# Cosine attention and a two-layer network on one core: the first chunk's second products in pairs of groups, and w_out loaded by whole rows

## The chip, the cores and the metric

The kernel runs on one core of a Trainium2 chip. The metric is the device time of one execution in microseconds (us); a profiled execution also gives a trace, whose span runs from the first to the last instruction. The engines of the core are named as in the profile: PE (matrix products, with PEld for the loading of weights), DVE (vector), ACT (activations), POOL (GpSimd), SP (which here only issues DMAs). Each runs its own instructions in order, and waits on semaphores for the others.

## What is computed

```python
q_n = q / (norm(q) + 1e-6);  k_n = k / (norm(k) + 1e-6)      # (8, 12, 448, 64)
attn = softmax(q_n @ k_n.T / 0.1)
x = (attn @ v).transpose(0, 2, 1, 3).reshape(3584, 768)
h = x @ w_in                                                  # (768, 2048)
out = maximum(0.01 * h, h) @ w_out                            # (2048, 768)
```

All inputs and the output are float32 in memory; the products run in bfloat16.

## The kernel before

**Slots.** Two heads make a slot, so a batch has 6 slots and there are 48 in all. A slot's q and k are loaded by SP (`load_qk`: four DMAs, the last two small; the first six slots by `load_first`), squared on POOL (`squares`, L184), summed on DVE (`sums`, L195), turned into norms on ACT (`roots`, L202 and L203), and scaled on DVE (`normalise`, L222 to L227). Its seven tiles are then transposed, on PE for slots below 10 and by a DMA on SP from slot 10 on (`transposes`, L259). `norm(s)` is roots, normalise, transposes, the load of a later slot, and the squares of slot s+2. `hold(x)` is a tiny copy on POOL that reads x, so what follows on POOL stands behind x.

**Scores and attention.** `key_tiles` makes one score tile (a pair of PSUM banks, L284) for each slot and key tile, and ACT takes its exp out of the banks (L296). `attend` and `attend_two` multiply the exps with v and with ones and scale the result into xT.

**The two layers.** A batch is a chunk of tokens (3 or 4 tiles of 128). `firsts` makes the 16 parts of the hidden layer (L388), each through one bank, with a Prelu on ACT into hT (L395). `visit` makes the second products (`two_groups`, L460): a group is one token tile and one half (384) of the 768 columns. Two groups run together in two banks, one on rows 0 to 63 of the contraction and one on rows 64 to 127; after all 16 m they change rows. A yield after each m (a step) lets `visit` put score tiles of the next batch and norms of later slots between them, at fixed steps (`three`, `four`, `norms`). In the first chunk (b = 0) the pairs are ((0,0),(1,0)), ((2,0),(0,1)), ((1,1),(2,1)), each (token tile, half). The other chunks have pairs ((ts,0),(ts,1)).

**Banks.** PSUM has eight banks. `banks` gives out the single bank or the pair that was used longest ago, apart from those kept for a group or a product.

**Loads.** POOL issues the loads of v, w_in (four) and w_out in the opening (`bulk`); DMAs of one issuing engine share a queue (q0 in the profile is POOL's, q1 is SP's). w_out comes as columns 0 to 383 in two loads of 8 m and then columns 384 to 767 in four loads of 4 m.

**The opening.** Slots 0 to 5 go one by one through squares, sums, roots, normalise, transposes and scores, written out by hand, with filler matmuls (`fill`) between. On POOL the order is: hold for slot 0's q, the first v load, hold for slot 0's remainder, the remainder loads of slots 3 to 5, hold for the scaled slot 0, squares of slot 2. For slots 0 and 1 the 1e-6 is added on ACT by an Identity (L205), for the others on DVE (L222).

The work of PE is one sequence in program order:

```python
attend(NQ - 1, ...); firsts(0, ...)
for b in range(B):
    visit(b, ...)            # second products of b, scores of b + 1
    attend_batch(b + 1)
    firsts(b + 1, 0, ...)
```

Of the kernel before, what the change touches and what calls it, by code (L numbers as in the profile page):

```python
# [8 lines left out]
F32 = mybir.dt.float32  # L9
# [7 lines left out]
def kernel(  # L17
# [10 lines left out]
    nc = tc.nc  # L28
# [47 lines left out]
    def banks(count, keep=None, which=None):  # L76
        lo, hi = (0, 8) if not deals["apart"] else (0, 4) if count == 2 else (4, 8)
        x = which if which is not None else min(
            (i for i in range(lo, hi, count) if not set(range(i, i + count)) & set(sum(kept.values(), []))),
            key=lambda i: max(age[i : i + count]),  # L80
        )
        deals["n"] += 1
        age[x : x + count] = [deals["n"]] * count
        if keep:
            kept[keep] = list(range(x, x + count))
        return ps[:, x] if count == 1 else ps[:, x : x + count]
# [20 lines left out]
            out=w_in_sb[:, e::2, n0 : n0 + D_ff // 2], in_=w_in_r[e, :, :, n0 : n0 + D_ff // 2]  # L107
        )

    def load_w_out(half, parts=1):  # L110
        n0, n = half * HALF, MT // parts
        for m in range(0, MT, n):
            gp.dma_start(
                out=w_out_sb[:, m : m + n, n0 : n0 + HALF],
                in_=w_out_r[:, m : m + n, n0 : n0 + HALF],
            )

    def main(x, b, h0, nh):
        return x[b, h0 : h0 + nh, 0:MAIN].rearrange("h (p t) d -> p h t d", t=3)
# [79 lines left out]
    def roots(s):  # L199
        if s >= NSLOT:  # L200
            return
        nc.scalar.activation(ss[s], ss[s], func=AF.Ln, bias=tiny)  # L202
        nc.scalar.activation(ss[s], ss[s], func=AF.Exp, scale=0.5)  # L203
        if s < 2:
            nc.scalar.activation(ss[s], ss[s], func=AF.Identity, bias=eps)  # L205

    qn, scalings = {}, {}

    def behind(eng, ins, why):

        tc.add_manual_dep(
            eng.nop().ins, ins.ins.name,
            mybir.DependencyInfo(mybir.DependencyClass.Sync, mybir.DependencyReason.DATA),
            reason=why,
        )

    def normalise(s):
        if s >= NSLOT:
            return
        r = smp.tile([128, 14], F32, name="r")  # L220
        if s >= 2:
            nc.vector.tensor_scalar_add(ss[s], ss[s], 1e-6)  # L222
        nc.vector.reciprocal(r, ss[s])  # L223
        qn[s] = qnp.tile([128, 7, 2, D], BF16, name="qn")
        for x, lo, hi, r0 in ((raw[s][0], 0, 4, 0), (raw[s][1], 4, 7, 8)):
            nt = hi - lo
            scalings[s] = nc.vector.tensor_tensor(  # L227
                qn[s][:, lo:hi],
                x.rearrange("p h t d -> p t h d"),
                r[:, r0 : r0 + 2 * nt].rearrange("p (h t) -> p t h", h=2)  # L230
                .unsqueeze(3).to_broadcast([128, nt, 2, D]),
                op=ALU.mult,
            )
# [209 lines left out]

    halves_done = {}

    def two_groups(c, two, last):

        po2 = banks(2, ("rows", c, two))  # L450
        done = {}
        for n in range(2):
            before, done = done, {}
            for m in range(MT):
                for h in range(2):
                    rows, i = slice(64 * h, 64 * h + 64), h ^ n
                    ts, half = two[i]
                    if n == 1 and m == 0:
                        behind(nc.tensor, before[i], "the other rows' products in this bank")
                    done[i] = nc.tensor.matmul(  # L460
                        out=po2[:, i, :HALF],
                        lhsT=hT[c][rows, m, ts * 128 : (ts + 1) * 128],
                        rhs=w_out_sb[rows, m, half * HALF : (half + 1) * HALF],
                        start=(n == 0 and m == 0), stop=(n == 1 and m == MT - 1),
                    )
                yield
        for i, (ts, half) in enumerate(two):
            if (c, ts) not in osb:
                osb[c, ts] = osp.tile([128, D_model], F32, name="osb")
            copy = nc.scalar.copy if last and i == 0 else nc.vector.tensor_copy  # L470
            copy(out=osb[c, ts][:, half * HALF : (half + 1) * HALF], in_=po2[:, i, :HALF])  # L471
            halves_done[c, ts] = halves_done.get((c, ts), 0) + 1
            if halves_done[c, ts] == 2:
                store(osb[c, ts], c, chunk_cols(c)[0] + ts * 128, 0, D_model)
        given_back(("rows", c, two))

    for part in range(2):
        load_first(nc.sync, q, part, 0, 1)
# [5 lines left out]
            load_first(nc.sync, x, part, s, n)  # L484
    tiny = cpool.tile([128, 1], F32, name="tiny")
    nc.vector.memset(tiny, 1e-18)
    eps = cpool.tile([128, 1], F32, name="eps")
    nc.vector.memset(eps, 1e-6)
    warm = cpool.tile([128, 512], BF16, name="warm")
    nc.vector.memset(warm, 1.0)  # L490
    ones = cpool.tile([128, 32], BF16, name="ones")
# [23 lines left out]
        seen = smp.tile([128, 1], F32, name="seen")  # L515
        gp.tensor_copy(out=seen, in_=x)  # L516

    hold(raw0[:, 0, 0, 0, 0:1])
    load_v(0)
    hold(raw0[:, 0, 0, 3, 0:1])  # L520
    for x in (q, k):
        load_first(gp, x, 1, 3, 3)


    (q_h, k_h), (q_h1, k_h1) = raw[0], raw[1]
# [19 lines left out]
    load_v_rem(0, slice(0, 2))  # L545
    dst = qtp.tile([128, 7, 128], BF16, name="qkT")
    qkT[0] = dst.rearrange("p t c -> p (t c)")
    for lo, hi, copy in ((0, 4, nc.scalar.copy), (4, 7, nc.vector.tensor_copy)):
        tp = transposed()
        one(tp, 0, lo, hi)  # L550
        if hi == 7:
            sums(1, (1,))
        copy(out=dst[:, lo:hi], in_=tp[:, lo:hi])
    fill(3)
    sums(1, (0,))
    sums(2, (0,))
    roots(1)
# [2 lines left out]
    def bulk(s):  # L560

        if s == 0:
            load_v(1)
            load_w_in(0)
        elif s == 1:
            load_v_rem(0, slice(2, 4))
            load_w_in(1)
        elif s == 2:
            load_v(2)
            load_w_in(2)  # L570
        elif s == 3:
            load_w_in(3)
            load_w_out(0, 2)
        elif s == 4:
            load_w_out(1, 4)

    def scaled(s):

# [150 lines left out]
    def visit(b, order, norms, between):  # L729


        s0 = (b + 1) * NPAIR
        tiles = [(s0 + p, ki) for p in range(NPAIR) for ki in range(3)]
        key_tiles([(s0 + 1, 3), (s0 + 3, 3)])
        for i, two in enumerate(order):
            after = between[i == len(order) - 1]
            for n, _ in enumerate(two_groups(b, two, i == len(order) - 1), 1):
                for _ in range(after.get(n, 0)):
                    key_tiles([tiles.pop(0)])
                for fn in norms.get((i, n), ()):  # L740
                    fn()
        assert not tiles
        key_tiles([(s0 + 5, 3)])

    three = ({5: 1, 11: 1, 16: 2, 21: 1, 27: 1}, {3: 1, 7: 1, 11: 1, 16: 2, 20: 1})
    four = ({5: 1, 11: 1, 16: 2, 24: 1}, {6: 1, 16: 2})

    deals["apart"] = False
# [16 lines left out]
    for b in range(B):  # L765
        tokens = chunk_cols(b)[1] // 128
        if b == B - 1:
            for ts in range(tokens):
                for half in range(2):
                    second(b, ts, half)  # L770
            break
        order = [((ts, 0), (ts, 1)) for ts in range(tokens)]
        if b == 0:
            order = [((0, 0), (1, 0)), ((2, 0), (0, 1)), ((1, 1), (2, 1))]
        norms = {(0, 16): [lambda: sums(11)], (0, 26): [lambda: norm(11)]}
        if b:
            norms = {}
            for i in range(tokens - 1):
                norms[i, 4] = [lambda s=ready + i: norm(s)]
                norms[i, 20] = [lambda s=ready + i + 1: sums(s)]  # L780
        visit(b, order, norms, three if tokens == 3 else four)
        ready += tokens - 1
        attend_batch(b + 1)
        for j in range((b + 2) * NQ, (b + 3) * NQ):
            load_v(j)
        load_v_rem(b + 2)
        s = ready
        between = {0: [lambda s=s: norm(s)], 1: [lambda s=s: sums(s + 1)]}
        if b == 0:
            between = {  # L790
                0: [lambda: sums(13)], 1: [lambda: norm(13), lambda: sums(14)],
                4: [lambda: norm(14), lambda: sums(15)], 7: [lambda: norm(15)],
                13: [lambda: sums(16)],
            }
            ready += 4
        elif tokens == 3:
            between.update({
                4: [lambda s=s: norm(s + 1), lambda s=s: sums(s + 2)],
                7: [lambda s=s: norm(s + 2), lambda s=s: sums(s + 3)],
                10: [lambda s=s: norm(s + 3)], 13: [lambda s=s: sums(s + 4)],  # L800
            })
            ready += 4
        else:
            between.update({
                4: [lambda s=s: norm(s + 1)], 5: [lambda s=s: sums(s + 2)],
                8: [lambda s=s: norm(s + 2)], 12: [lambda s=s: sums(s + 3)],
            })
            ready += 3
        firsts(b + 1, 0, between)
# [35 lines left out]
```

## Time and profile before

| | us |
|---|---|
| median of 3 runs (lowest, highest) | 409.29 (409.26, 409.75) |
| the profiled execution | 408.97 |
| its span | 407.2 |
| PE busy | 399.3 (98%) |
| ACT busy | 262.6 (64%) |
| DVE busy | 189.8 (47%) |
| POOL busy | 140.7 (35%) |
| second products L460: busy, mean of one | 143.2, 323 ns |
| score exps L296: mean of one | 919 ns |

The durations of the trace come from the one profiled execution; 1.8 us of its time lie outside the span. Where the profile names a wait, the text in square brackets gives the idle time of the engine before an instruction and what ended it. Of two lines of DMA queues, the first number is packets, the second MB written, the third the time that the packets took as a share of 16 DMA engines; several packets can be under way on an engine, so a share can be over 100%.

### The profile page before, as it was taken

How to read it: one execution, taken by the hardware profiler on the slowest of the kernel's cores; microseconds unless marked ns; L12 is line 12 of the kernel's file. 1: busy time of each engine (PE TensorE's matmuls, PEld its weight loads, DVE VectorE, ACT ScalarE, POOL GpSimd, SP SyncE). 2: the span in 40 equal slices, each digit the busy share in tenths (PEclk: the TensorE clock that was granted, in tenths of full speed). 3: DMA queues.
4: the chain of work that ended last, by engine and by line, in shares of the span. 5: the costliest groups of instructions: out<-in, count | busy, mean ns of one | idle time of the engine just before them, and what ended most of it. 6: DMA issues, size and time to landing. Idle time of an engine off the chain costs nothing.

```text
span 407.2 us, 10112 instructions
## 1 busy us (share of the span) xinstructions
PE 399.3 (98%) x4096; PEld 216.3 (53%) x4096; DVE 189.8 (47%) x405; ACT 262.6 (64%) x455; POOL 140.7 (35%) x215
## 2 busy tenths in 40 slices
PE   7899999999999999999999999999999999999996
PEld 2335657544555655544555555544555555554564
DVE  6887951771645624354542635256261645130021
ACT  4996598565865688744876569845876559944300
POOL 4995461471323522343231614055231530000000
PEclk9999999999999999999999999999999999999999
DMA  7999999694595659378385848486476833210033
GB/s 169 263 212 218 222 181 212 194 211 107 134 208 82 142 85 218 65 117 174 78 196 121 131 119 146 130 117 136 93 194 142 111 74 63 63 41 2 0 77 79
DMA packets 104175, 54.21 MB, mean 133 GB/s; under 512 B 70016, under 2 KB 99072, under 8 KB 104128
## 3 DMA queue, kind: packets, MB, share of 16 engines
q1 hardware_dynamic: 78064, 41.04, 43.6%
q0 software_dynamic: 25216, 12.00, 24.0%
q8 instruction: 32, 0.52, 0.6%
q10 hardware_dynamic: 848, 0.52, 0.5%
q14 instruction: 15, 0.12, 0.1%
HBM read 45.61 MB, written 11.01 MB: 139 GB/s over the span
## 4 chain that ended last, share of the span: by engine, by line
PE 93%; DMA 3%; DVE 1%; POOL 1%; SPq 1%; issue 0%
PE ps L388 36%; PE ps L460 31%; PE ps L324 11%; PE ps L284 8%; PE ps L425 5%; DMA raw<-in_k_dram 2%; PE ps L311 1%; DMA raw<-in_q_dram 1%; DMA qk<-in_q_dram 1%; DVE qn L227 1%; PE ps L241 1%; POOL sq L184 1%; DVE ss L195 0%; SPq L129 0%; SPq L134 0%
## 5 line engine op out<-in xcount | busy, mean ns | idle before, releaser
L388 PE MATMUL ps<-xT,w_in_sb 128*128 128x384 bf16 (+1 forms) x768 | 148.0, 353 | 0.0
L460 PE MATMUL ps<-w_out_sb,hT 64*128 64x384 bf16 x1536 | 143.2, 323 | 0.0
L296 ACT ACTIVATE pe<-ps 128x896 bf16<-128x896 f32 x144 | 123.3, 919 | 19.5 <-PE ps L284 17.8
L395 ACT ACTIVATE hT<-ps 128x384 bf16<-128x384 f32 (+1 forms) x128 | 67.4, 543 | 70.1 <-PE ps L388 69.7
L388 PEld LDWEIGHTS <-w_in_sb 128*128 128x128 bf16 x768 | 74.1, 98 | 71.7 <-issue 4.0
L460 PEld LDWEIGHTS <-hT 64*128 64x128 bf16 x1536 | 76.4, 94 | 52.9 <-issue 2.7
L184 POOL TENSOR_TENSOR sq<-qk 128x512 f32<-128x512 f32 x84 | 77.3, 940 | 17.6 <-DMA qk<-in_k_dram 17.0
L284 PE MATMUL ps<-qkT 64*128 64x448 bf16 (+1 forms) x384 | 55.1, 354 | 1.6 <-ACT pe L296 0.9
L195 DVE TENSOR_REDUCE ss<-sq 128x6 f32<-128x384 f32 (+1 forms) x95 | 54.5, 610 | 2.9 <-POOL sq L184 2.8
L471 DVE COPY osb<-ps 128x384 f32<-128x384 f32 x41 | 21.3, 553 | 72.9 <-PE ps L460 42.4
L516 POOL CAST seen<-qn 128x1 f32<-128x1 bf16 x47 | 8.8, 187 | 127.3 <-DVE qn L227 122.7
L227 DVE TENSOR_TENSOR qn<-qk,r 128x512 bf16<-128x512 f32 x84 | 50.5, 642 | 1.7 <-DVE r L223 0.3
L222 DVE TENSOR_SCALAR ss<-ss 128x14 f32<-128x14 f32 x46 | 9.9, 214 | 67.9 <-ACT ss L203 67.8
L365 DVE TENSOR_TENSOR xT<-ps,rb 128x448 bf16<-128x448 f32 x48 | 27.7, 619 | 26.5 <-ACT rb L344 26.3
L162 POOL DMA_DIRECT2D v_b<-in_v_dram x24 | 18.7, 784 | 54.2 <-PE ps L324 54.2
L324 PE MATMUL ps<-pe,v_b 128*32 128x448 bf16 x576 | 32.0, 353 | 0.0
L284 PEld LDWEIGHTS <-qkT 64*128 64x128 bf16 (+1 forms) x384 | 17.0, 96 | 20.5 <-issue 8.5
L431 DVE COPY osb<-ps 128x384 f32<-128x384 f32 (+1 forms) x9 | 4.6, 513 | 36.6 <-issue 22.6
L324 PEld LDWEIGHTS <-v_b 128*32 128x32 bf16 x576 | 15.1, 97 | 11.9 <-issue 0.6
L343 ACT ACTIVATE rb<-ps 128x448 f32<-128x448 f32 x24 | 12.9, 537 | 13.2 <-PE ps L324 12.2
L296 ACT ACTIVATE pr<-ps 128x896 bf16<-128x896 f32 x24 | 21.3, 919 | 0.2 <-PE ps L284 0.2
L425 PE MATMUL ps<-w_out_sb,hT 128*128 128x384 bf16 (+1 forms) x144 | 21.0, 308 | 0.0
(52 smaller groups left out, 201.2 us busy)
## 6 DMA issues: line engine op xcount, KB each, us to landing
qk<-in_q_dram SPq DMA_DIRECT2D x42, 192.0 KB, 3.5
qk<-in_k_dram SPq DMA_DIRECT2D x42, 192.0 KB, 3.6
out_dram<-osb SPq DMA_DIRECT2D x30, 192.0 KB, 2.9
v_b<-in_v_dram POOLq DMA_DIRECT2D x24, 192.0 KB, 4.9
out_dram<-osb SPq DMA_DIRECT2D x12, 384.0 KB, 2.6
w_in_sb<-in_moe_w_in_dram POOLq DMA_DIRECT2D x4, 768.0 KB, 11.4
w_out_sb<-in_moe_w_out_dram POOLq DMA_DIRECT2D x2, 768.0 KB, 21.3
w_out_sb<-in_moe_w_out_dram POOLq DMA_DIRECT2D x4, 384.0 KB, 24.8
```

The lines of the kernel that those rows point to most:

```text
L184: eng.tensor_tensor(sq, x, x, op=ALU.mult)
L195: nc.vector.tensor_reduce(o.rearrange("p (h t) -> p h t", h=2), sqs[s][i], axis=AX.X, op=ALU.add)
L227: scalings[s] = nc.vector.tensor_tensor(qn[s][:, lo:hi], x.rearrange("p h t d -> p t h d"), r[:, r0 : r0 + 2 * nt].rearrange("p (h t) -> p ...
L284: nc.tensor.matmul(out=out[:, a, :S], lhsT=x[rows, c0:c1], rhs=x[rows, 0:S], start=True, stop=True,)
L296: nc.scalar.activation(out=dst, in_=sc[:, :, :S], func=AF.Exp, scale=inv_tau)
L324: nc.tensor.matmul(out=x[32 * g : 32 * g + 32, :S], lhsT=weights(g, ki) if ki < 3 else rem(g), rhs=pe[s][:, ki, a, :] if ki < 3 else pr[j] ...
L365: nc.vector.tensor_tensor(xT[m][:, 2 * jj + e, half * S : (half + 1) * S], pos.pop((j, e))[:, :S], rbs[j], op=ALU.mult,)
L388: nc.tensor.matmul(out=pm[:, :n], lhsT=w_in_sb[:, kt, m * 128 : (m + 1) * 128], rhs=xT[c // 2][:, kt, c0 : c0 + n], start=(kt == 0), stop= ...
L395: nc.scalar.activation(out=hT[c][:, m, :n], in_=pms.pop((c, m))[:, :n], func=AF.Prelu, alpha=0.01)
L425: nc.tensor.matmul(out=po2[:, :n], lhsT=hT[c][:, m, ts * 128 : (ts + 1) * 128], rhs=w_out_sb[:, m, lo : lo + n], start=(m == 0), stop=(m = ...
L460: done[i] = nc.tensor.matmul(out=po2[:, i, :HALF], lhsT=hT[c][rows, m, ts * 128 : (ts + 1) * 128], rhs=w_out_sb[rows, m, half * HALF : (ha ...
L471: copy(out=osb[c, ts][:, half * HALF : (half + 1) * HALF], in_=po2[:, i, :HALF])
```

## The change

- `load_w_out` loads four parts of 4 m, each with all 768 columns, in place of two loads of 8 m and four of 4 m by half columns.
- `two_groups` becomes `groups`, which takes several pairs of groups and a number of parts. In the first chunk two pairs, ((0,0),(0,1)) and ((1,0),(1,1)), run together in four banks, with m in four parts: in each part first pair, second pair, then both again with the rows changed. The third pair ((2,0),(2,1)) follows alone, in one part, as all pairs of the other chunks do. Before each change of rows the weights wait for the last products of that pair.
- The score tiles of the long group of 64 steps stand at the steps of `wide`.
- The 1e-6 is added on DVE for all slots; the Identity on ACT and its constant go.
- Slot 0's second transposed part is copied on ACT behind the first; slot 1's two sums follow each other on DVE behind it.
- On POOL the first hold goes and the first v load moves behind the remainder loads of slots 3 to 5.

```diff
-    def load_w_out(half, parts=1):
-        n0, n = half * HALF, MT // parts
-        for m in range(0, MT, n):
-            gp.dma_start(
-                out=w_out_sb[:, m : m + n, n0 : n0 + HALF],
-                in_=w_out_r[:, m : m + n, n0 : n0 + HALF],
-            )
+    def load_w_out(parts):
+        for m in parts:
+            gp.dma_start(out=w_out_sb[:, m : m + MT // 4], in_=w_out_r[:, m : m + MT // 4])
...
-        if s < 2:
-            nc.scalar.activation(ss[s], ss[s], func=AF.Identity, bias=eps)
...
-        if s >= 2:
-            nc.vector.tensor_scalar_add(ss[s], ss[s], 1e-6)
+        nc.vector.tensor_scalar_add(ss[s], ss[s], 1e-6)
...
+    def groups(c, pairs, parts, last):
+        pos2 = [banks(2, ("rows", c, two)) for two in pairs]
+        done = [{} for _ in pairs]
+        per = MT // parts
+        for x in range(2 * parts):
+            part, n = divmod(x, 2)
+            for p, two in enumerate(pairs):
+                if x:
+                    for i in range(2):
+                        behind(nc.tensor, done[p][i], "the other rows' products in this bank")
+                for m in range(part * per, (part + 1) * per):
+                    for h in range(2):
+                        rows, i = slice(64 * h, 64 * h + 64), h ^ n
+                        ts, half = two[i]
+                        done[p][i] = nc.tensor.matmul(
+                            out=pos2[p][:, i, :HALF],
+                            lhsT=hT[c][rows, m, ts * 128 : (ts + 1) * 128],
+                            rhs=w_out_sb[rows, m, half * HALF : (half + 1) * HALF],
+                            start=(n == 0 and m == 0), stop=(n == 1 and m == MT - 1),
+                        )
+                    yield
+        for po2, two in zip(pos2, pairs):
...
-    hold(raw0[:, 0, 0, 0, 0:1])
-    load_v(0)
     hold(raw0[:, 0, 0, 3, 0:1])
     for x in (q, k):
         load_first(gp, x, 1, 3, 3)
+    load_v(0)
...
-    for lo, hi, copy in ((0, 4, nc.scalar.copy), (4, 7, nc.vector.tensor_copy)):
+    for lo, hi in ((0, 4), (4, 7)):
         tp = transposed()
         one(tp, 0, lo, hi)
-        if hi == 7:
-            sums(1, (1,))
-        copy(out=dst[:, lo:hi], in_=tp[:, lo:hi])
+        nc.scalar.copy(out=dst[:, lo:hi], in_=tp[:, lo:hi])
     fill(3)
+    sums(1, (1,))
     sums(1, (0,))
...
-            load_w_out(0, 2)
+            load_w_out((0, 4))
         elif s == 4:
-            load_w_out(1, 4)
+            load_w_out((8, 12))
...
+    wide = (dict.fromkeys((5, 10, 16, 21, 26, 32, 37, 42, 48, 53, 58, 63), 1), three[1])
...
-            order = [((0, 0), (1, 0)), ((2, 0), (0, 1)), ((1, 1), (2, 1))]
+            order = [order[0] + order[1], order[2]]
...
-        visit(b, order, norms, three if tokens == 3 else four)
+        visit(b, order, norms, wide if b == 0 else three if tokens == 3 else four)
```

## The prediction

> **What bounds the kernel now.** I read the chain of waits first: the tensor engine (PE) carries 93% of it, and in order of time it leaves the other engines for good when the transposed copy of slot 4 ends at 25.3 us.
>
> ```profile
> PE 93%; DMA 3%; DVE 1%; POOL 1%; SPq 1%; issue 0%
> ```
>
> ```profile
> 24.69 0.61 DVE qkT L265
> 25.34 0.36 PE ps L284 x2
> ...
> 51.27 0.50 PE ps L284 x8
> 51.77 0.92 PE ps L460 x10
> ```
>
> So the change can act in two ways: through the opening (before 25.3 us), or by making PE wait later, where every wait is paid in full because PE has no idle time to give it from.
>
> The second view is the timeline around the opening and around 50 us, where the first chunk's second products begin.
>
> ```profile
> 7.28 0.24 DVE L223 RECIPROCAL r<-ss 128x14 f32<-128x14 f32 x1 [0.96 <-ACT ss L205]
> 9.55 1.04 POOL L184 TENSOR_TENSOR sq<-raw 128x512 f32<-128x512 f32 x1 [0.58 <-DMA raw<-in_q_dram]
> 10.93 2.51 ACT L296 ACTIVATE pe<-ps 128x896 bf16<-128x896 f32 x3
> ```
>
> ```profile
> 48.41 2.01 POOL L184 TENSOR_TENSOR sq<-qk 128x512 f32<-128x512 f32 x2 [3.21 <-DMA qk<-in_k_dram]
> ...
> 49.90 1.14 DVE L195 TENSOR_REDUCE ss<-sq 128x8 f32<-128x512 f32 x2
> ...
> 51.06 0.31 ACT L202 ACTIVATE ss<-ss,tiny 128x14 f32<-128x14 f32 x1 [0.25 <-DVE ss L195]
> ...
> 51.89 1.71 ACT L296 ACTIVATE pr<-ps 128x896 bf16<-128x896 f32 x2
> ...
> 52.52 0.35 PE L284 MATMUL ps<-qkT 64*128 64x448 bf16 x2
> ```
>
> What to see in it: the squares of slot 10 wait 3.21 us for their q and k load; its sums follow, then its roots (L202) in ACT's queue, already 0.25 us late. ACT works in order, so behind the roots stand the last Prelu of the chunk (L395, at 51.52) and the exps that free score banks (L296). Load to PE is one chain with no slack.
>
> The third view is the DMA queues by window: 34 to 38 us (w_in, packets of 2,048 B written, beside q and k loads), 42 to 50 us (w_out, 768 B), and 40 to 42 us (w_out nearly alone). Columns: packets, MB, share.
>
> ```profile
> q0 software_dynamic: 332, 0.66, 86.6%
> q1 hardware_dynamic: 331, 0.24, 24.6%
> ```
>
> ```profile
> q0 software_dynamic: 1306, 0.99, 78.6%
> q1 hardware_dynamic: 1298, 0.80, 44.5%
> ```
>
> ```profile
> q0 software_dynamic: 518, 0.40, 127.5%
> q1 hardware_dynamic: 44, 0.01, 4.1%
> ```
>
> While both have work, the two queues move the same number of packets, whatever their sizes. So the size of a packet on POOL's queue (q0) sets the pace of SP's (q1), which carries q and k.
>
> **The change part by part.**
>
> (a) The opening. Slots 0 and 1 lose an Identity on ACT (0.31 us, L205) and gain an add on DVE (about 0.2, L222): slot 0's reciprocal at 7.28 comes about 0.14 earlier. The copy of tiles 4 to 6 moves from DVE (0.36) to ACT behind the other one (0.58): first scores +0.2, but DVE gets to slot 1's sums 0.4 sooner. The first v load (0.94 of POOL) moves behind two remainder loads; its packets no longer share the engines with the load that the squares at 9.55 wait for (0.58 of waiting, which could go). From there a loop squares, sums, normalise runs at 3.6 to 3.9 us a slot to 25.3, so the gain carries through: -0.5, bounds -0.7 and +0.2. But w_in's second load, issued at 19.96 with 10.3 us to landing, is there at 30.26; PE uses it from 30.5 (L388, 30.51). It lies in a queue that is full from 10 us on, with the same bytes ahead of it, so only -0.25 of it passes. The v load's first use is at 20.58, so its 3.4 us delay is covered.
>
> (b) Two pairs of groups keep four of the eight banks. Score tiles then have two bank pairs in place of three. In the chain six steps of the group are 0.97 us and a tile is 0.19; a hand-over between engines is 0.05 there. The tile after step 5 (52.52 now, into a third pair) must wait for the first pr exp: 51.89 + 0.92 + 0.05 = 52.86, that is +0.34. Within the long group tiles are 1.0 to 1.35 us apart and a pair is needed after two of them, against 0.35 (matmul) + 0.92 + 0.10 = 1.37: covered. At its end two tiles (after steps 58 and 63) hold both pairs: the last group's first products wait for the one (1.35 of PE work against 1.37: +0.02), and the tile after its step 3 for the other (0.86 against 1.37: +0.51). Together +0.53; bounds 0 and 0.8, as no row shows two pairs alone.
>
> (c) w_out by whole rows. Same bytes, but packets of 768 columns x 2 B = 1,536 B where they had 384 columns, 768 B. From the windows one packet of each queue takes, on each of 16 engines, 16 x 8 us / 1,302 = 98 ns with 768 B and 16 x 4 / 331 = 193 ns with 2,048 B; in between by bytes, 1,536 B gives 155 ns. The load of slot 10 is 2 x 256 + 2 x 128 = 768 packets, 48 an engine: 48 x 98 ns = 4.7 us now, 48 x 155 = 7.4 then. All of it lies behind w_in (window 40 to 42: hardly a q1 packet), so it is wholly beside w_out. Its last part now lands at 48.25 (issued 39.85, 8.4 to landing). It lands 2.7 us later then; it is issued some 0.2 earlier through (a), so +2.5. Bounds: 0 (engines share by bytes) and 48 x 95 ns = 4.6 (w_in's pace). I take 2.5 as 1,536 B lies between two measured sizes. Hence slot 10's roots at 53.56 in place of 51.06, Prelu and exps behind them in ACT's queue equally late, and the tile after step 5 at 52.86 + 2.5 = 55.36 against 52.52: +2.84 with (b)'s 0.34 in it. (a)'s gain ends in this wait. The matmul of the second pair in the first bank that the last Prelu empties is held too, inside the same wait.
>
> (d) The load of slot 11 follows. Now it lands at 53.16 (last issue 42.87, 10.3 to landing); twice the 2.7 less the 0.2 makes 58.4 us. Its sums end 2.4 us behind (now 53.32 to 55.73): 60.9; ACT comes to its roots at 57.49 + 2.84 = 60.3 and waits 0.6, which the spare of the two bank pairs takes. Its DMA transpose (2.3 us behind the roots, 7.7 to landing) lands at 60.9 + 2.3 + 7.7 = 70.9; its first tile (67.55 now) comes at 70.95. I take 0, bounds 0 and +1.5.
>
> (e) At nothing: 12 more switches of the row halves wait for matmuls 8 places back, 0.65 us against 0.32. w_out's four parts are needed at about 51.8, 55, 59 and 63 plus the delay, with the last landing near 60.5 as now: no wait, and now there is none either, so nothing is won. POOL issues four w_out DMAs for six (4.8 us of issuing becomes about 3.2), where it idles 4.45 us before 38.34 anyway. Output copies of the two pairs stand together on DVE at the long group's end, where DVE is mostly idle; SP's stores keep their order. Without that cover each copy would cost 0.55.
>
> Sum: 2.84 + 0.53 = +3.4 us. The profiled execution has a span of 407.2 and 1.8 around it, 408.97: 412.4 by it. The median is 409.29, 0.3 above it: **412.7 us**.
>
> **The rivals.**
>
> More (414.7): a load that comes new stands behind packets already taken: slot 10's is issued at 38.3 and hardly moves before 42, some 20 packets of w_in. With 20 larger w_out packets (by bytes 120 ns against 62) that is up to +1.2, and slot 11's transpose adds 0.8: +2.0. For it: the 3.4 us of standing still. Against: those packets are w_in's, which stay as they are. The Trainium skill, DMA: Bandwidth & Descriptors, "Queues, rings and completion order", says an engine changes queues only after a packet of about 9 to 17 descriptors; equal counts agree with turns, but no row shows a turn's length, and longer turns would speak for this rival.
>
> No change (409.9): engines share by bytes and the equal counts are chance, so (c) is 0: -0.25 + 0.34 + 0.53 = +0.6. Decides if slot 10's squares begin by about 48.5. Against it: two windows with two sizes of packet and counts equal within 1%.
>
> Faster (408.8): the opening is worth more. If the queue is not full at 6 to 12 us (only 173 GB/s in 6 to 9.4), taking the v load out lets everything behind it, w_in included, land sooner: 0.7 from the squares, 0.4 from DVE's copy, 0.3 from the Identity, -1.4, with (b) +0.9 against it: -0.5. It also needs (c) at 0; decides if w_in's second load lands before 29.3.
>
> The change does what it says in any case: the changed program's order has the 64-step group, four w_out loads and ACT's copy in it.
>
> **How the numbers follow.** Forecast 0.62, more 0.16, no change 0.13, faster 0.09. A measurement tells 0.2% (0.8 us) from nothing. Slower 0.79 (the first two and the edge of the third), same 0.12, faster 0.09. Range 409.7 to 414.7: out of it lie the faster case and about 0.06 above. The forecast's own range, from (c)'s bounds narrowed to 1.5 to 3.5 and (b)'s and (d)'s, is 411.3 to 414.2.
>
> **What would show it.** In 42 to 50 us both queues move some 820 packets each, not 1,300; slot 10's squares begin near 51, its roots near 53.5, with ACT idle before them; PE idles 2 to 3 us near 52.5 for Prelu and exps, and 0.5 where the last group begins; the opening's unbroken PE run begins about 0.5 before 25.3. I am wrong if 42 to 50 still has 1,300 q1 packets, or if the squares come late and PE does not idle.

## The result and the profile after

The changed kernel takes 413.48 us (median of 5, 412.98 to 413.99) against 409.39 (median of 5, 409.26 to 410.11) on the same chip: ratio 1.0098, 95% interval 1.0086 to 1.0111, 4.1 us slower. The profiled executions have spans of 411.6 and 407.2 us, 4.4 apart. Lines of the changed kernel lie 4 to 7 above those of before: w_in's products L388 are L381, w_out's products L460 are L456, roots L202/203 are L198/199, exps L296 are L289, Prelu L395 is L388, squares L184 are L180.

The page of the changed kernel, its granted clock in 40 slices, the shares of the chain of waits by engine, and one of the groups:

```profile
PEclk9999989999999999999999999999999999999999
...
PE 88%; DMA 5%; DVE 2%; POOL 1%; issue 1%; ACT 1%; SPq 1%; POOLq 0%
...
L456 PE MATMUL ps<-w_out_sb,hT 64*128 64x384 bf16 x1536 | 144.8, 325 | 2.1 <-ACT hT L388 2.1
```

PE has fallen from 93 to 88% of the chain and DMA risen from 3 to 5: the chain now leaves PE a second time, after the opening. One group of products has 2.1 us of idle time before it, and the sixth slice has a lower clock. The chain in order of time shows the place (start, length, what):

```profile
39.07 11.32 DMA qk<-in_k_dram
...
53.00 0.32 ACT ss L198
53.32 0.02 issue
53.34 0.21 ACT ss L199
53.56 0.38 ACT hT L388
53.93 0.82 ACT pr L289
54.75 0.04 issue
54.79 0.56 PE ps L277 x2
```

and the timeline of the same stretch, with the waits in brackets:

```profile
50.56 1.82 POOL L180 TENSOR_TENSOR sq<-qk 128x512 f32<-128x512 f32 x2 [5.81 <-DMA qk<-in_k_dram]
51.06 0.82 PE L456 MATMUL ps<-w_out_sb,hT 64*128 64x384 bf16 x8
...
53.98 0.34 PE L456 MATMUL ps<-w_out_sb,hT 64*128 64x384 bf16 x2 [2.10 <-ACT hT L388]
54.79 0.56 PE L277 MATMUL ps<-qkT 64*128 64x448 bf16 x2 [0.47 <-ACT pr L289]
```

Slot 10's load lands at 50.40 (48.25 before), its roots start at 53.00 (51.06), and the last Prelu and the exps stand behind them. PE does four steps of the long group, then waits 2.10 us for the bank that the last Prelu empties and 0.47 for an exp. The tile behind step 5 comes at 54.79 where it came at 52.52: +2.27.

The DMA queues from 42 to 50 us (packets, MB, share), where before there were 1,306 and 1,298 packets:

```profile
q0 software_dynamic: 856, 1.27, 86.7%
q1 hardware_dynamic: 857, 0.48, 27.8%
```

So the two queues still go packet for packet, at the pace of the larger packets. Behind the wait comes what I had not foreseen. Windows of two stretches (length; busy time of PE, then weight loads, DVE, ACT and POOL, each with its number of instructions in brackets; then the granted clock, DMA share, GB/s):

```profile
51.28:54.70 3.42, 0.94 (x10) 0.34 (x7) 2.28 (x6) 1.67 (x5) 1.23 (x3) 1.00 1.15 224
54.70:58.11 3.41, 3.32 (x22) 1.77 (x23) 0.54 (x2) 2.41 (x4) 0.00 (x0) 0.50 1.51 201
```

From 54.70 to 58.11 the clock is 0.50 and PE does 22 matmuls where the next stretch of equal length, at clock 1.00, has 44. Matched product by product, the changed kernel is 2.27 us late before this stretch and 3.88 behind it: 1.6 us more. The record of before has no such drop. At the last group's start one more wait brings the lag to 4.4, and there it stays to the end:

```profile
69.28 0.36 PE L277 MATMUL ps<-qkT 64*128 64x448 bf16 x2 [0.34 <-ACT pe L289]
```

2.27 + 1.6 + 0.5 = 4.4. The theory to be tested: the larger packets of w_out delay slot 10; the idle time made by that halves the clock; the two waits for banks are the rest; the opening's gain ends in the wait for slot 10. Rivals: the long group costs by itself; the reordered opening loads do; the half clock has another cause.

### The profile page after: what moved, and what is told of

Read it like the earlier page. It is cut to its first block, busy times and chain, and to the rows that moved or that the text cites. A ratio compares the mean times of both kernels' runs of the same rounds, so it can differ in the third digit from the quotient of the medians.

```text
span 411.6 us, 10137 instructions
## 1 busy us (share of the span) xinstructions
PE 402.1 (98%) x4096; PEld 215.8 (52%) x4096; DVE 189.6 (46%) x405; ACT 263.4 (64%) x454; POOL 139.0 (34%) x212
## 4 chain that ended last, share of the span: by engine, by line
PE 88%; DMA 5%; DVE 2%; POOL 1%; issue 1%; ACT 1%; SPq 1%; POOLq 0%
PE ps L381 32%; PE ps L456 30%; PE ps L317 11%; PE ps L277 8%; PE ps L418 5%; DMA qk<-in_k_dram 3%; DMA raw<-in_q_dram 2%; PE ps L304 1%; DVE qn L220 1%; POOL sq L180 1%; DVE ss L191 0%; DVE r L216 0%; DVE xT L358 0%; ACT pe L289 0%; ACT pr L289 0%
## 5 line engine op out<-in xcount | busy, mean ns | idle before, releaser
L381 PE MATMUL ps<-xT,w_in_sb 128*128 128x384 bf16 (+1 forms) x768 | 148.2, 353 | 0.0
L456 PE MATMUL ps<-w_out_sb,hT 64*128 64x384 bf16 x1536 | 144.8, 325 | 2.1 <-ACT hT L388 2.1
L289 ACT ACTIVATE pe<-ps 128x896 bf16<-128x896 f32 x144 | 124.2, 918 | 21.0 <-PE ps L277 18.8
L388 ACT ACTIVATE hT<-ps 128x384 bf16<-128x384 f32 (+1 forms) x128 | 67.4, 543 | 70.4 <-PE ps L381 70.0
L381 PEld LDWEIGHTS <-w_in_sb 128*128 128x128 bf16 x768 | 74.0, 98 | 71.9 <-issue 4.0
L456 PEld LDWEIGHTS <-hT 64*128 64x128 bf16 x1536 | 75.4, 95 | 57.2 <-issue 5.2
L180 POOL TENSOR_TENSOR sq<-qk 128x512 f32<-128x512 f32 x84 | 77.3, 941 | 20.4 <-DMA qk<-in_k_dram 19.5
L289 ACT ACTIVATE pr<-ps 128x896 bf16<-128x896 f32 x24 | 21.2, 918 | 0.2 <-PE ps L277 0.2
```

The source lines that it names most:

```text
L180: eng.tensor_tensor(sq, x, x, op=ALU.mult)
L289: nc.scalar.activation(out=dst, in_=sc[:, :, :S], func=AF.Exp, scale=inv_tau)
L381: nc.tensor.matmul(out=pm[:, :n], lhsT=w_in_sb[:, kt, m * 128 : (m + 1) * 128], rhs=xT[c // 2][:, kt, c0 : c0 + n], start=(kt == 0), stop= ...
L388: nc.scalar.activation(out=hT[c][:, m, :n], in_=pms.pop((c, m))[:, :n], func=AF.Prelu, alpha=0.01)
L456: done[p][i] = nc.tensor.matmul(out=pos2[p][:, i, :HALF], lhsT=hT[c][rows, m, ts * 128 : (ts + 1) * 128], rhs=w_out_sb[rows, m, half * HAL ...
```

## The experiments

Each run was timed beside the kernel before on the same chip; its median there is given with the ratio.

**Half columns.** w_out's parts again in packets of 768 B, all else as changed.

```diff
-            gp.dma_start(out=w_out_sb[:, m : m + MT // 4], in_=w_out_r[:, m : m + MT // 4])
+            for n0 in (0, HALF):
+                gp.dma_start(out=w_out_sb[:, m : m + MT // 4, n0 : n0 + HALF],
+                             in_=w_out_r[:, m : m + MT // 4, n0 : n0 + HALF])
```

> The changed kernel, but each of w_out's four parts is loaded in two transfers of 384 columns, so its packets are 768 B again; the order of the products, the banks and the opening stay as changed. If the larger packets are what costs: between 42 and 50 us the two queues go back from some 857 packets each to about 1,300 each, slot 10's last load lands at about 48 us instead of 50.4, its roots start at 50.5 to 51 instead of 53.0, the tensor engine does not idle 2.1 us before 54, the granted clock stays at 1.0, and the time is 409.0 to 409.9 (the opening's 0.64 against 0.85 of waits for banks). If the long group of two pairs costs by itself (its banks, its switches of rows), the packets change nothing and the time stays at 412.5 to 413.7. If the half clock came from something other than the stall, the loads are early, the record still shows 0.5 near 55 us, and the time is near 411.

412.46 (before: 409.76), ratio 1.0066 [1.0054, 1.0078]. Slot 10's load landed early, at 48.34, and the clock stayed at 1.0 through the long group, but the time did not come back. The timeline of GpSimd (POOL) in this run tells why:

```profile
37.58 0.74 POOL L113 DMA_DIRECT2D w_out_sb<-in_moe_w_out_dram  x1 [3.77 <-DMA w_in_sb<-in_moe_w_in_dram]
41.41 0.74 POOL L113 DMA_DIRECT2D w_out_sb<-in_moe_w_out_dram  x1 [3.09 <-DMA w_in_sb<-in_moe_w_in_dram]
```

POOL's transfers report on eight semaphores in turn. With eight transfers for w_out instead of four, the seventh and eighth wait for w_in's last two loads, which held the same semaphores, and slot 8's and 9's squares stand behind them in POOL's queue. Slot 9's squares (L184) start at 44.21 instead of 41.59, and slot 10's roots at 53.98: late again, from another cause. Before that, at 30.95, PE had also waited 0.98 us for w_in's second load, which landed at 30.90 here (29.78 in the changed kernel). The run decides nothing about the time; it only shows that the packets set when the load lands.

**Two transfers later.** The same, with the last two issued behind slot 9's squares, when those semaphores are free.

```diff
-            load_w_out((8, 12))
+            load_w_out((8,))
...
     norm(7, False)
+    load_w_out((12,))
```

> As the run with half columns, but the last two of the eight transfers are issued only behind slot 9's squares, so that GpSimd no longer stands before them from 33.8 to 41.4 us. If the packets are the cause and the blocked GpSimd was the other wait: slot 10's load lands at 48.0 to 48.6, its roots start at 50.8 to 51.3, the tile behind step 5 comes at 52.5 to 53.1 (after: 54.79), no clock drop, and the time is 410.0 to 410.9 against 409.76 before (the opening's gain is eaten by slot 10's chain, and the wait at the last group's start, 0.5, stays). If the long group costs by itself: the load is early, but the time stays above 412.

409.70 (before: 409.51), ratio 1.0001 [0.9992, 1.0010]: the whole 1% is gone, more than I expected (410.0 to 410.9). The DMA windows, 42 to 50 us, and the timeline, slot 10's squares on POOL and the tile behind step 5:

```profile
q0 software_dynamic: 1341, 1.00, 79.5%
q1 hardware_dynamic: 1338, 0.77, 44.0%
```

```profile
47.52 1.90 POOL L184 TENSOR_TENSOR sq<-qk 128x512 f32<-128x512 f32 x2 [2.96 <-DMA qk<-in_k_dram]
...
51.96 0.36 PE L281 MATMUL ps<-qkT 64*128 64x448 bf16 x2 [0.17 <-ACT pr L293]
```

The load landed at 47.36, 0.6 earlier than I expected, the roots started at 50.17, and no wait of PE over 0.2 is left there.

**The control.** Whole rows as changed, with only the last transfer issued later (the diff just above on the changed kernel).

> The control for the run with half columns and two later transfers: the changed kernel with whole rows (packets of 1,536 B) and only the last of the four transfers issued later, behind slot 9's squares. If the size of the packets is the cause: slot 10's load lands at 50 to 51 us again, and the time stays at 413.0 to 414.0. If the later issue itself gave the 3.8 us: 409.5 to 410.5.

413.36 (before: 409.27), ratio 1.0096 [1.0079, 1.0113], as expected if the packets are the cause. The windows from 42 to 50 us are again those of the changed kernel, and so are POOL's squares:

```profile
q0 software_dynamic: 856, 1.27, 86.6%
q1 hardware_dynamic: 857, 0.48, 27.8%
```

```profile
50.53 1.82 POOL L180 TENSOR_TENSOR sq<-qk 128x512 f32<-128x512 f32 x2 [5.89 <-DMA qk<-in_k_dram]
```

The three runs together: the later issue by itself does nothing, the size of the packets makes the 4 us, and the long group with its banks and switches of rows, in the run with small packets, costs no more than the opening gains (0.89 us ahead of before at its first product, 0.01 ahead behind the wait at the last group's start).

**A fifth buffer.** Slot 10's load need not wait for slot 6's buffer; w_out stays in whole rows.

```diff
-    ldp = ctx.enter_context(tc.tile_pool(name="ld", bufs=4))
+    ldp = ctx.enter_context(tc.tile_pool(name="ld", bufs=5))
...
-    warm = cpool.tile([128, 512], BF16, name="warm")
+    warm = cpool.tile([128, 256], BF16, name="warm")
```

> The changed kernel with five buffers for Q and K instead of four, so that slot 10's load no longer waits for slot 6's buffer and goes out right behind slot 9's, ahead of most of w_out (the warm-up products read 256 columns twice instead of 512 once, to make room). If the late landing of slot 10 is the cause of both the stall and the half clock: its last load lands before 46 us, its roots start at 50.5 to 51, no clock drop, and the time is 409 to 410 with w_out still in whole rows, unless w_out's later parts now hold the tensor engine (they landed at 50.6, 55.8 and 59.9, and are wanted at about 55, 58.5 and 62 us). If the whole rows cost in another way, it stays at 412.5 to 414.

410.63 (before: 409.76), ratio 1.0020 [1.0010, 1.0029]. Most of the loss is gone without touching the packets, though not all that I expected (409 to 410). The load, issued at 31.37 instead of 39.07, landed at 48.96, not before 46: in SP's queue it stands behind slot 9's (landed at 41.41), and 48 packets an engine at the 149 ns measured with whole rows (16 x 8 us / 856) are 7.2 us from there, 48.6. PE still waits, but short enough for the clock to stay at 1.0:

```profile
52.55 0.34 PE L456 MATMUL ps<-w_out_sb,hT 64*128 64x384 bf16 x2 [0.83 <-ACT hT L388]
53.35 0.36 PE L277 MATMUL ps<-qkT 64*128 64x448 bf16 x2 [0.47 <-ACT pr L289]
```

**The old opening.** The changed kernel with before's opening: the Identity on ACT, the copy on DVE and the order of the first v load as they were.

```diff
+        if s < 2:
+            nc.scalar.activation(ss[s], ss[s], func=AF.Identity, bias=eps)
...
+    for lo, hi, copy in ((0, 4, nc.scalar.copy), (4, 7, nc.vector.tensor_copy)):
...
+    hold(raw0[:, 0, 0, 0, 0:1])
+    load_v(0)
     hold(raw0[:, 0, 0, 3, 0:1])
```

> The changed kernel with the opening as it was before (the first two slots' 1e-6 added on the scalar engine, the second half of the first transposes copied by the vector engine, V's first load ahead of the remainder loads). If the opening's gain ends in the wait for slot 10's load: the first chunk's second products start 0.5 to 0.7 us later, but slot 10's roots start within 0.3 of 53.0 and the time is 413.2 to 413.9, the same as the changed kernel. If the opening's gain is passed on to the end, the time is 414.0 to 414.3. If the reordered opening loads are part of what delays slot 10, the time falls below 413.

413.17 (before: 409.76), ratio 1.0079 [1.0059, 1.0099]: as the changed kernel, within the intervals. So the new opening's loads are not the cause, and a gain of the opening can't be told in this time. The profile is of the slowest execution (414.74: slot 10's load at 51.69, roots at 54.30, each 1.3 later than expected), so the times of single steps can't be held against the expectation; slot 10's load was issued 1.27 later than in the changed kernel (40.34 for 39.07) and landed 1.29 later, so an earlier issue does pass to the landing. The six executions lie in two groups, 412.06 to 412.37 with a mean clock of 0.998 to 1.000, and 413.96 to 414.74 with 0.995 to 0.996, the mean that one stretch of 3.4 us at 0.5 makes.

**The opening alone**, on the kernel before (the diff's opening hunks, nothing else).

> The kernel before with nothing but the new opening. If the opening is worth what the start of the first chunk's second products showed (0.64 us), and w_out's first half (which landed at 51.92, behind the start at 51.70) still comes in time: 408.6 to 409.1. If w_out's landing, or slot 10's load, takes it up: 409.2 to 409.5, no change. If it costs something later: above 409.6.

409.73 (before: 409.76), ratio 1.0007 [0.9989, 1.0025], no change. Ten of twelve executions took 408.83 to 410.56, two 412.27 and 412.77. The profile is of the last, and shows what the old order of loading has no cover for:

```profile
62.63 0.94 PE L457 MATMUL ps<-w_out_sb,hT 64*128 64x384 bf16 x7 [2.50 <-DMA w_out_sb<-in_moe_w_out_dram]
```

There w_out's last quarter of a half landed at 62.59 (60.46 in the profile of before), PE waited 2.50, and from 63.18 on the clock was 0.5 for 3.4 us. The load was issued 1.03 earlier than in before (32.08 for 33.11) and took 3.2 us longer to land; why isn't shown, and what takes up the gain in the ten quicker executions is in no trace.

**The wait filled.** The changed kernel with eight useless products in front of the long group.

```diff
+        if len(pairs) > 1:
+            for i in range(8):
+                nc.tensor.matmul(out=pos2[0][:, 0], lhsT=warm[:, :128], rhs=warm,
+                                 start=(i == 0), stop=(i == 7))
```

> The changed kernel with eight products of 128x512 ones (0.21 us each, 1.7 in all) put on the tensor engine ahead of the long group, into the first pair's bank, which is written anew behind them: useless work that fills most of the wait for slot 10. Slot 10's load and roots stay at 50.4 and 53.0. If the half clock is made by the idle time and costs 1.6 us: the record shows no 0.5 near 55 us, the wait before the second pair's first products falls from 2.10 to about 0.4, and the time falls to 411.6 to 412.4 although work was added. If the clock has nothing to do with the idle time, or costs nothing: 413 to 414 with the same 0.5 in the record. If the fill displaces the chain: above 414.

412.02 (before: 409.51), ratio 1.0062 [1.0045, 1.0079]: 1.5 us less than the changed kernel's median, with 1.7 us of products more. Windows of the stretches that answer to the two above:

```profile
51.72:55.13 3.41, 3.00 (x25) 1.24 (x19) 2.18 (x5) 1.56 (x4) 1.32 (x3) 1.00 1.15 225
55.13:58.55 3.42, 3.22 (x40) 2.21 (x41) 0.64 (x2) 3.22 (x5) 0.00 (x0) 1.00 1.60 180
```

PE is busy 3.00 of 3.41 instead of 0.94, and the clock behind it is 1.00. Product by product this execution is 2.80 us behind the kernel before at the place where the changed one is 3.88, although its slot 10 load landed 0.53 later (50.93): less that, 1.6 us for the clock. Its total, 414.02, is the highest of six (four are 411.62 to 412.20); slot 11's load landed at 60.37 instead of 58.07, and at full clock PE then waited 1.55 for it at 64.39. That is the price that I had as the upper bound for slot 11.

**What halves the clock.** The kernel before, with one wait of PE in each of seven chunks, of rising length, then of about one length.

```diff
+    def stall(k):
+        wm = banks(1)
+        nc.tensor.matmul(out=wm, lhsT=warm[:, :128], rhs=warm, start=True, stop=True)
+        for i in range(k):
+            x = nc.scalar.activation(out=idle, in_=wm[:, :448], func=AF.Prelu, alpha=0.01)
+        behind(nc.tensor, x, "a wait of the wanted length")
...
+        between.setdefault(9, []).append(lambda: stall(1 + b))
         firsts(b + 1, 0, between)
```

> The kernel before, with one wait of the tensor engine in each of the chunks 1 to 7, behind the products of column block 8: one product of ones, then 1, 2, ... 7 scalar-engine instructions of 448 columns on it (about 0.45 to 0.55 us each), and the tensor engine waits for the last: idle times of about 0.6, 1.1, 1.6, 2.1, 2.6, 3.1 and 3.6 us. If idle time within a window of about 3.4 us halves the clock: the waits up to 1.1 show no drop, those from 2.6 on show a drop to 0.5 of 3.4 us length behind them, with 1.6 between; each drop costs up to 1.7 us on top of its wait. If only a whole idle window does it: no drop up to 3.1, and the changed kernel's drop had another cause.

> As the run with waits of rising length, but with seven waits of one length, about 2.5 us each (four scalar-engine instructions). In that run 2.53 and 3.68 halved the clock and 3.21 did not; counted from the start of the clock's record in steps of 3,413 ns, every drop began at a step's end, and the step before it held 2.07 us of idle or more, while none with up to 1.87 did. If it is the share of one step of that grid that decides: of the seven equal waits those with over 2.07 us inside one step are followed by a drop at that step's end, those split with less than 1.87 on both sides are not; by the lengths some four of seven should drop. If the length of the wait alone decides: all seven drop, or none.

The two runs took 435.29 and 436.40 us (one execution each). Both expectations of a mere length fell with the first run: 2.53 us halved the clock, 3.21 did not. Laid on a grid of 3,413 ns from the start of each record of the clock, all drops behind these waits begin at a line of the grid and last one step. Windows of the second run, one step of the grid to a line, around its second and third wait:

```profile
143.07:146.49 3.42, 0.89 (x6) 0.32 (x5) 2.69 (x6) 3.15 (x8) 1.77 (x4) 1.00 0.84 190
146.49:149.90 3.41, 3.41 (x11) 1.54 (x12) 0.00 (x0) 0.49 (x1) 1.10 (x2) 0.50 0.79 193
190.86:194.27 3.41, 2.72 (x13) 1.05 (x11) 2.32 (x6) 2.42 (x6) 1.54 (x4) 1.00 0.78 193
194.27:197.69 3.42, 1.47 (x7) 0.70 (x8) 0.32 (x1) 1.80 (x4) 1.42 (x2) 1.00 0.78 191
197.69:201.10 3.41, 3.41 (x17) 1.56 (x16) 2.24 (x6) 2.20 (x5) 0.51 (x2) 1.00 0.13 26
```

A wait of 2.53 inside one step leaves it 0.89 of work, and the next step has 0.50. A wait of 2.64 cut by a line leaves 2.72 and 1.47, and nothing happens. All fourteen (idle worked out from PE's matmul records):

| wait, us | idle in its fullest step | clock halved behind it |
|---|---|---|
| rising: 1.38, 1.38, 2.06 | 1.22, 1.37, 1.15 | no, no, no |
| rising: 2.53, 3.21, 3.68, 4.36 | 2.45, 1.65, 3.00, 3.41 | yes, no, yes, yes |
| equal: 2.53 (three of them) | 2.53 each | yes, yes, yes |
| equal: 2.92, and three of 2.64 | 2.02, 1.94, 1.87, 1.79 | no, no, no, no |

Of the seven equal waits three halved the clock, where I expected some four; the four others lie at 2.02 or below in their fullest step. Among steps whose products use all 128 rows, 2.02 is the most idle without a drop, and the least with one is 2.07, in the last full step of the first run. The changed kernel's drop had 2.47 of idle in its step. One number for all steps does not come out: the control with whole rows dropped behind a step with 1.90, in which all products use 64 of the 128 rows.

**All three mended, and the tiles moved.** First a fifth buffer, small packets and later tiles together (the last group's at 5, 10, 14, 18, 18, 22); then, on the run with two transfers later, only the tiles, as in this diff; then that with the buffer.

```diff
-    wide = (dict.fromkeys((5, 10, 16, 21, 26, 32, 37, 42, 48, 53, 58, 63), 1), three[1])
+    wide = (dict.fromkeys((8, 13, 18, 23, 28, 32, 37, 42, 47, 52, 57, 62), 1), {5: 1, 8: 1, 12: 1, 16: 2, 20: 1})
```

> The changed kernel with what the runs point to: a fifth buffer for Q and K (slot 10's load goes out behind slot 9's), w_out in packets of 768 B with the last two transfers issued later, the first tile of the long group behind step 8 instead of 5, and the last group's tiles behind steps 5, 10, 14, 18, 18, 22 instead of 3, 7, 11, 16, 16, 20. If slot 10's chain and the two waits for banks are all that stands against the opening's gain of 0.64: no idle of the tensor engine over 0.2 us between 51 and 72 us, no clock drop, and 408.9 to 409.4 against 409.76 before. If something else of the long group costs: 409.8 or more. If w_out's parts now come late: waits of the second products for w_out at about 54, 58 or 61 us.

> The run with half columns and two later transfers, with only the tiles of scores moved: in the long group behind steps 8, 13, 18 ... 62 instead of 5, 10, 16 ... 63, in the last group behind 5, 8, 12, 16, 16, 20 instead of 3, 7, 11, 16, 16, 20 (step 16, where the rows switch, keeps its two tiles: moved away from there in the run with all three, the switch waited 0.16 and its step took 0.49). That run lost 0.32 at the long group's first tile and 0.5 at its end out of a lead of 0.89. If these are waits for banks and nothing else: no idle of the tensor engine over 0.1 us between 50 and 72 us, the lead of 0.6 to 0.9 reaches the end, and the time is 0.5 to 0.9 below before (some 408.7 to 409.1). If the tiles' exponentials only wait elsewhere: the same as before within 0.3.

> The same with the fifth buffer for Q and K besides (slot 10's load issued behind slot 9's; warm-up products of 256 columns). If slot 10's chain still decides anything (its roots stood 0.25 behind the sums): 0.1 to 0.3 below the run without the buffer. If not: the same; if the smaller warm-up or the earlier load disturbs w_in's second load (landed at 29.7 there, 30.2 in the run with all three): 0.3 above it.

All three: 409.46 (before 409.51), ratio 1.0001 [0.9991, 1.0010]. Tiles only: 409.29 (before 409.50), 0.9989 [0.9978, 1.0000]. With the buffer: 409.38, 0.9991 [0.9977, 1.0005]. None gave the gain of 0.4 to 0.9 that I expected of the first two. In the profile of the run with only the tiles moved, both waits for banks are gone; the longest left from 27 to 72 us are for transfers:

```profile
30.36 0.66 PE L385 MATMUL ps<-xT,w_in_sb 128*128 128x384 bf16 x3 [0.33 <-DMA w_in_sb<-in_moe_w_in_dram]
...
67.89 0.55 PE L281 MATMUL ps<-qkT 64*128 64x448 bf16 x4 [0.37 <-DMA qkT<-qn]
```

There the opening was 0.75 ahead, w_in's second load (landed at 30.32) let 0.24 of it pass, and behind the wait for slot 11's transposed tile (landed at 67.84) the run was 0.35 late. Slot 10's chain makes no wait there any more, and the buffer changes nothing in the time, though in its profile w_in's second load, at 30.46, cost PE 0.89. This is the best version found; its interval ends at 1.0000, so it is before's equal or 0.2% better.

## Why the prediction was right, and where it was not

The forecast was 412.7, the range 409.7 to 414.7; measured 413.48. The direction, the cause and the place were right, and one term was missing. That the forecast lies so near is in part luck: the chain and the banks, predicted at +3.4, came to 2.8 in the trace, and the missing term to 1.6.

- **(c), the packets: right, but for the time of issue.** Predicted some 820 packets a queue and 155 ns for a pair of them; measured 856 and 149 ns. In the traces slot 10's 768 packets begin at 41.95 before and 41.18 after, and the last of them starts 4.73 and 7.30 us later (predicted 4.7 and 7.4). From the last issue to landing the load took 2.93 us longer (11.33 for 8.40, predicted 2.7), but it was issued 0.78 earlier, not 0.2, so it landed 2.15 later, not 2.5. The roots came 1.94 later. The step that failed is the small one: "it is issued some 0.2 earlier".
- **(b), the banks: right.** The tile behind step 5 came 2.27 later (predicted 2.84, with (c) in it). Of the wait, 2.10 falls already on the second pair's first products, whose bank the last Prelu empties, as named at the end of (c); 0.47 on the tile. In the run with two later transfers, where slot 10 is early, this tile cost 0.32 (predicted 0.34). At the last group's start I predicted 0.53 and it cost 0.5.
- **(a), the opening: the gain was undersized, its end wrong.** The unbroken run of PE starts 0.93 earlier, not 0.5: squares of slot 2 wait for nothing now and start at 8.67 instead of 9.55. "With the same bytes ahead of it" failed for w_in's second load: it was issued 0.94 earlier and landed 0.48 earlier (29.78), so 0.78 passed, not 0.25. "(a)'s gain ends in this wait" failed with it: slot 10's load was issued 0.78 earlier and its packets began 0.77 earlier, so the wait ends that much earlier. In the run with two later transfers the lead went into the waits for banks, in the one with the tiles moved into w_in's second load and the last group, where slot 11's transpose was waited for.
- **(d), slot 11: right in the changed kernel** (landed at 58.07, predicted 58.4; no wait). Its sums end at 60.64 and its roots start at 61.79; without the 1.6 us of the clock ACT would have come to them at 60.2, by estimate, and waited 0.5, near the 0.6 that I had. The profile of the filled run shows that the cover is thin: there the load landed 2.3 us later, PE was back at full clock, and 1.55 was waited.
- **(e): right.** No run shows a cost of the switches in the long group, or a wait for w_out in its new order. It may be worth more than nothing: in one profile of the old order a wait of 2.50 for w_out was seen, in those of the new one none.
- **The missing term: the clock.** My sum took PE to resume at full speed behind a wait of 2 to 3 us. In the profiled execution that cost 1.6 us, the rest of the 4.4. It does not come in every execution: three of five timed ones of the changed kernel have a mean clock of 0.996 (413.39 to 413.99), two 1.000 (412.98 and 413.48). These two are not 1.6 faster, and what they lose instead is not in a trace; a wait for slot 11 at full clock, as in the filled run's profile, is one candidate. So the 1.6 is shown for the profiled execution, and for the median it stays open.
- **The rivals.** "More" lies near in time, but by its own mechanism it is refuted: from the load's first issue to its first packet slot 10 stood still for 3.7 us in both kernels (38.27 to 41.95, 37.49 to 41.18), so larger packets added nothing there, and slot 11's transpose made no wait. "No change" fell with the equal counts in a third size of packet. "Faster" asked for w_in before 29.3; it landed at 29.78, and even the opening alone gave nothing in the median.

## What to carry to other kernels

Where two DMA queues alternate by packets, making one queue's packets longer slows the loads on the other; before loading weights by whole rows, see what comes in on the other queue at that time and who waits for it. When costing a stall of the tensor engine of about 2 us or more, add up to 1.7 us for a halved clock, and expect it in some executions only. A gain in an opening that is bound by transfers has to be followed to each later landing before it is counted.

## What the runs showed of the hardware

- Behind these waits the tensor engine's clock is halved for one step of 3,413 ns, on a grid that starts at another point in each execution (4.1 to 7.5 us after the span's start in these). Three waits of 2.53 us inside one step halved it; one of 3.21, cut by a line of the grid so that neither step held more than 1.65 of idle, did not.
- The Trainium skill, "TensorE: Matmul & The Clock Gate", section "Part 1: The HAM clock gate", gives a free-running window of 3,413 ns: every drop here agrees. Its section "HAM oscillation" asks only for no idle gaps beyond about 3.4 us; here it differs, since 2.47 us of idle in one window (the wait of 2.10 and most of that of 0.47) were enough. The measurement decides.
- With three sizes of packet on POOL's queue (768, 1,536 and 2,048 B) the counts of the two queues, while both had work, stayed equal within 1%, at 98, 149 and 193 ns for a pair.
- Useless work can pay: 1.7 us of products in a stall that had to be waited out anyway made the kernel 1.5 us faster.
